# Four buffers for gathered rows instead of two, and all copies of transposed rows on ScalarE, in a fused attention and top-1 expert kernel

## The chip, the cores and the metric

The kernel runs on one core of a Trainium2 chip. A core has five engines that run side by side and wait for each other by semaphores: TensorE (PE, matrix multiplication and transposes; its weight loads are shown apart, as PEld), VectorE (DVE), ScalarE (ACT), GpSimd (POOL) and SyncE (SP, which here only starts transfers). Matrix results arrive in PSUM, which is divided into eight banks; everything else that is computed on lies in SBUF. The metric is the device time of one execution, in microseconds (us).

## The reference

Two blocks are computed one after the other, all in 32-bit floats. First comes linear attention with decay, over 4 batches, 8 heads, 768 positions and heads of 64, in blocks with a running state. Its output, seen as 3072 tokens of 512 numbers, goes through a switch layer: a router picks one of 8 experts for each token, and that expert's two-layer network is applied.

```python
def _moe_ref(x, w_gate, w1, w2):          # x: 3072 x 512, w1: 8 x 512 x 1024, w2: 8 x 1024 x 512
    logits = x @ w_gate
    expert_idx = np.argmax(logits, axis=1)
    probs = softmax(logits)                # written out in the reference
    gate_w = probs[np.arange(N), expert_idx]
    for e in range(E):
        mask = expert_idx == e
        h = np.maximum(x[mask] @ w1[e], 0.0)
        out[mask] = gate_w[mask, None] * (h @ w2[e])
```

## The kernel before

**Attention and routing, 0 to about 140 us.** The positions are taken in six steps of 128, each for two pairs of batches. For each, PE transposes q and k, forms scores, applies them to v and updates the state. The attention output of 128 tokens is copied from PSUM by ACT (xT, line 286), multiplied with a matrix that turns it back and gives the router's logits (lines 319 and 321), copied by ACT again (lg and x, lines 325 and 326) and stored to the DRAM tensor xs. `choose` finds each token's expert. `put` counts with two small matmuls (rank, line 375) the place of each token on its expert's list and writes one entry per token to the DRAM tensor slots, with an indirect transfer from POOL (line 391).

**The expert passes.** The expert part works on lists of tokens in nine passes. Expert 0 is split: pass 0a takes its first 256 tokens, and its turn runs while attention still finishes, and pass 0b takes 136 more. Passes 1 to 7 take one whole expert each, with 424, 408, 408, 384, 368, 368 and 360 tokens. A pass has these steps:

- `fetch` (line 429) gathers the rows of the pass from xs into tiles xg, 128 rows per indirect transfer from POOL (line 437). One tile of xg holds two such blocks of rows, so a pass takes one tile (0a, 0b) or two (1 to 7). The tiles come from a pool with the tag xg.
- `turn` (line 461) transposes the rows on PE: for each of four chunks of 128 features there are one to four transposes into a PSUM bank (tp, line 466; two banks, 0 and 1, in turn), and the bank is then copied to the tile xgT. Copies of chunks 0 and 2 go to DVE (line 453), those of 1 and 3 to ACT (line 451), so chunk 2 waits for the copy of chunk 0, and chunk 3 for that of chunk 1.
- `hidden` (passes 0a and 0b, line 476) or `hidden_fast` (passes 1 to 7, line 552) multiplies with w1. `hidden_fast` uses a Strassen-like scheme of seven products on halves of the operands, in two rounds. It needs sums of halves of w1 (`first_sums`: the tiles s_k, s_q, s_v and one in place of a part of w1t, four POOL operations, lines 513 and 516) and of the tokens (`token_sums`: four DVE operations, lines 506 to 509, named t_sd, xgT, t_x, t_xT). DVE combines the products (lines 489 to 493 and 561), ACT applies the relu (line 563).
- `outputs` (line 611) and, for the first two blocks of 128 tokens of passes 1 to 7, `outputs_fast` (line 580) multiply with w2. The latter needs sums of w2 (`second_sums`: t_q, t_v, t_k, t_m, four POOL operations) and of the hidden values (`pair_sums`: h_qsT, h_qT, h_kT, h_kd, four DVE operations that read SBUF tiles, lines 499 to 502). The second of the seven products of line 580 reads t_k and h_kT.
- `scatter` (line 443) writes the rows to their places in the output, by indirect transfers from POOL.

**What sets the order.** The loop at line 788 works on pass i and prepares the next ones: after `hidden` of a pass come the turn of the next pass, its token sums, the first sums for it, the gathers for the pass after it, the second sums, and then the outputs of the current pass. So the turn of a pass stands between the hidden part and the outputs of the pass before it. Weights of a pass are loaded by SP two passes ahead, when the tiles w1t and w2t come free. The sums of weights share pools with the attention's inputs, three buffers for each of the tags q, k, v, so t_q of a pass takes the buffer that s_q of the pass before held, and can't start before PE is done with that s_q; the same goes for t_v and s_v.

The framework gives out the buffers of a tag in rotation, adds the waits for buffers and data, and reorders instructions within an engine by its own estimate of when they can start, except those that are pinned. Each engine then runs its list in order. With two xg tiles, a gather for the pass after the next waits until the next pass has been turned; on POOL's list everything behind such a gather waits with it.

Of the kernel before, what the change touches and what calls it, by code (L numbers as in the profile page):

```python
# [10 lines left out]
F32 = mybir.dt.float32  # L11
BF16 = mybir.dt.bfloat16
I32 = mybir.dt.int32
# [8 lines left out]
def kernel(  # L22
# [29 lines left out]
    nc = tc.nc  # L52
    B, H, S, D = q.shape
    N, MD = out.shape
    E = moe_w_gate.shape[1]
    F = moe_w1.shape[2]
    P = 128
# [13 lines left out]
    R = N + EARLY + P  # L71
    ENTRY = 4
# [112 lines left out]
    ffn = ctx.enter_context(tc.tile_pool(name="ffn", bufs=2))  # L185
# [3 lines left out]
    def bank(i, shape, name):  # L189
        return ps.tile(shape, F32, tag=f"bank{i}", name=name)  # L190
# [7 lines left out]
    def pin(inst):  # L198
        tc.keep_in_program_order(inst)
# [195 lines left out]
            tc.declare_no_dep(put.ins, group="put", reason="disjoint rows of the lists")  # L395
            tc.add_to_no_dep_group("put", put.ins)

    empty = ffn.tile([P, E * R // P, ENTRY], I32, tag="xg", name="empty", bufs=2)
    nc.gpsimd.memset(empty, 0)
    nc.gpsimd.memset(empty[:, :, 1], N)  # L400

# [18 lines left out]
    def at(m, t):  # L420

        w = m.widths[t]
        return m.ids[:w, t, 0:1], m.ids[:w, t, 1:2], m.list[:w, t, 2:3]
# [5 lines left out]
    def fetch(m, rows=1 + N):  # L429
        m.xg = []  # L430
        for t, w in enumerate(m.widths):
            if t % 2 == 0:
                m.xg.append(ffn.tile([P, 2, MD], F32, tag="xg", name="xg", bufs=2))
            gather(m.xg[-1][:w, t % 2, :], at(m, t)[0], rows)

    def gather(dst, idx, rows):
        nc.gpsimd.indirect_dma_start(  # L437
            out=dst, out_offset=None, in_=xs[:rows, :],
            in_offset=bass.IndirectOffsetOnAxis(ap=idx, axis=0))
# [6 lines left out]
        tc.declare_no_dep(put.ins, group="rows", reason="a token is on one list, once")  # L446
        tc.add_to_no_dep_group("rows", put.ins)

    def evac(i, dst, src):
        if i % 2:  # L450
            nc.scalar.copy(dst, src)
        else:
            nc.vector.tensor_copy(dst, src)

    def relu(i, dst, src):
        if i % 2:
            nc.scalar.activation(dst, src, ACT.Relu)
        else:
            nc.vector.tensor_scalar_max(dst, src, 0.0)  # L459

    def turn(m, pin=lambda inst: inst):
        m.xgT = ffn.tile([P, DC, m.n], F32, tag="xgT", name="xgT", bufs=1)
        for dc in range(DC):
            tp = bank(next(tp_banks), [P, m.n], "tp")
            for t, w in enumerate(m.widths):
                pin(nc.tensor.transpose(tp[:, t * P:t * P + w],  # L466
                                        m.xg[t // 2][:w, t % 2, dc * P:(dc + 1) * P],
                                        ident[:w, :w]))
            evac(dc, m.xgT[:, dc, :], tp)

    def hidden(m, w1t):
        m.hT = ffn.tile([P, FC, m.n], F32, tag="hT", name="hT", bufs=1)
# [215 lines left out]
    def start_early():  # L688

        nc.vector.tensor_scalar(out=skip, in0=had, scalar1=-1.0, scalar2=float(EARLY),  # L690
                                op0=ALU.mult, op1=ALU.add)
        nc.vector.tensor_scalar_max(skip, skip, 0.0)
        base[0] = const.tile([P, E], F32, name="ebase_late")
        nc.vector.tensor_copy(base[0], ebase)
        nc.vector.tensor_add(base[0][:, 0:1], base[0][:, 0:1], skip)
        m = make_pass(0, 0, EARLY, "0a")
        fetch(m, 1 + (NSTEP - 2) * B * C)
        passes.append(m)
# [11 lines left out]
    for i in range(len(order)):  # L710
# [20 lines left out]
        if ahead:  # L731
            for s in range(2):
                score(ahead, s)
        last, cur = cur, ahead
    turn(passes[0], pin)
    give_places(chosen.pop())
    leave(last)
# [47 lines left out]
    for m in passes[1:3]:  # L785
        fetch(m)
    last = len(passes) - 1
    for i, m in enumerate(passes):
        w1t, w2t = weights[max(i - 1, 0)]
        if i < 2:  # L790
            hidden(m, w1t)
        else:
            w1, w2 = w1_next, w2_next
            hidden_fast(m, w1)
        if 0 < i < last:
            turn(passes[i + 1])
            token_sums(passes[i + 1])
            w1_next = first_sums(weights[i][0])
        if 0 < i < last - 1:
            fetch(passes[i + 2])  # L800
        if 0 < i < last:
            w2_next = second_sums(weights[i][1])
        if i == last:

            tc.keep_in_program_order(nc.gpsimd.drain())
        if i < 2:
            outputs(m, w2t)
        else:
            outputs_fast(m, w2t, w2)
        if i == 0:  # L810
            turn(passes[1])
        if 0 < i < last - 1:
            weights.append(load_weights(passes[i + 2].w))
# [3 lines left out]
    with tc.If(most > 0):  # L817
        for i in range(E):
            tiles = nc.values_load(beyond[0:1, i:i + 1], min_val=0, max_val=MORE[i])
            with tc.If(tiles > 0):  # L820
# [4 lines left out]
                with tc.For_i(0, tiles, 1) as r:  # L825
                    m = SimpleNamespace(n=P, widths=[P])
# [36 lines left out]
```

## Time and profile before

| what | value |
|---|---|
| median of three runs | 477.9 us (477.66 to 478.23) |
| the profiled execution's own time | 476.67 us |
| its span, first to last instruction | 474.9 us |
| PE busy | 452.5 us, 95% |
| DVE, ACT, POOL busy | 215.2, 126.6, 247.4 us |
| copies of transposed rows on DVE (line 453) | 18, 9.2 us in all |
| the same on ACT (line 451) | 18, 8.1 us in all |
| gathers (line 437), passes 1 to 7 | 24, 25.8 us busy, 70.1 us idle before them |
| granted TensorE clock, mean | 0.993 |

Times in the text are us from the start of the span of the profiled execution. In a line of the timeline the first number is the start and the second the duration; then come the engine, the line of the kernel, the operation, the tiles written and read, their shapes, and how many instructions of the kind are merged. In square brackets stands how long the engine was idle before it and what ended the idle time. In a list of waits the three numbers are the total in us, how often, and the longest. A turn is named by the pass whose rows it turns: the turns of passes 0a, 0b and 1 to 7 begin on PE at 132.6, 164.6, 173.8, 206.5, 251.2, 294.2, 334.8, 372.7 and 410.5.

### The profile page before, as it was taken

The numbers are of one execution on the slowest core, as the hardware profiler recorded it, in microseconds if no ns is written. First come the engines' busy times: TensorE is split into PE (matmuls) and PEld (weight loads), VectorE is DVE, ScalarE is ACT, GpSimd is POOL, SyncE is SP. The second block draws the span as 40 slices with busy tenths as digits, with TensorE's granted clock in tenths as the row PEclk, the third lists the DMA queues.
The fourth block names the chain that finished last, engine by engine and source line by source line (L and its number), as shares of the span: only waits on it lengthen the run. The fifth ranks groups of instructions, "written<-read, shape, count | busy, mean of one in ns | idle before, by whom it ended". The sixth has DMA issues, their size and how long they took to land.

```text
span 474.9 us, 8613 instructions
## 1 busy us (share of the span) xinstructions
PE 452.5 (95%) x3447; PEld 375.5 (79%) x3447; DVE 215.2 (45%) x495; ACT 126.6 (27%) x323; POOL 247.4 (52%) x190
## 2 busy tenths in 40 slices
PE   5999999999899999999999999999999999999994
PEld 4889898988686475975995799599689689779963
DVE  3753656555433124471245435534623623653421
ACT  3453444544331011220122213112212212211310
POOL 5423535333144749949914970993596398621001
PEclk9999999999899999999999999999999999999998
DMA  9999999998214946441516060542615426001001
GB/s 180 229 268 244 215 241 228 256 303 282 85 54 122 305 153 216 153 181 68 201 48 245 26 222 15 227 141 107 239 41 203 181 78 224 1 20 44 1 17 51
DMA packets 99840, 72.60 MB, mean 153 GB/s; under 512 B 81235, under 2 KB 81239, under 8 KB 99792
## 3 DMA queue, kind: packets, MB, share of 16 engines
q1 hardware_dynamic: 90608, 52.49, 40.1%
q0 software_dynamic: 5008, 13.16, 7.9%
q10 hardware_dynamic: 4176, 6.31, 3.8%
q8 instruction: 29, 0.48, 0.4%
q14 instruction: 19, 0.16, 0.1%
HBM read 58.88 MB, written 13.16 MB: 152 GB/s over the span
## 4 chain that ended last, share of the span: by engine, by line
PE 89%; SPq 3%; DMA 2%; DVE 2%; issue 1%; ACT 1%; POOL 0%; POOLq 0%; ACTq 0%
PE p L552 27%; PE p L580 18%; PE po L611 16%; PE op L277 4%; PE sp L242 4%; PE ph L476 3%; SPq L93 3%; PE tp L466 3%; PE op L265 3%; PE tx L319 2%; PE cp L294 2%; PE tk L207 2%; PE tx L321 2%; PE tq L207 2%; DMA k_in<-in_k_dram 2%
## 5 line engine op out<-in xcount | busy, mean ns | idle before, releaser
L611 PE MATMUL po<-w2t,hT 128*128 128x512 f32 (+5 forms) x224 | 81.0, 596 | 0.0
L437 POOL DMA_INDIRECT xg<-xs,list x24 | 25.8, 1075 | 70.1 <-PE tp L466 64.6
L611 PEld LDWEIGHTS po<-w2t,hT 128*128 128x128 f32 (+5 forms) x224 | 30.5, 162 | 38.2 <-issue 37.9
L563 ACT ACTIVATE hT<-hT 128x408 f32<-128x408 f32 (+4 forms) x56 | 29.5, 527 | 86.7 <-DVE hT L561 86.0
L443 POOL DMA_INDIRECT out_dram<-o,list x24 | 23.8, 990 | 50.9 <-DVE o L617 27.7
L232 POOL TENSOR_TENSOR kd<-k_in,kdec 128x512 f32<-128x512 f32 x20 | 20.7, 1056 | 40.1 <-PE cp L294 22.3
L552 PE MATMUL p<-xgT,w1t 128*128 128x204 f32 (+4 forms) x224 | 41.5, 328 | 0.0
L391 POOL DMA_INDIRECT slots<-entry,slot_i x24 | 23.3, 973 | 31.4 <-DMA w2t<-in_moe_w_dram 12.4
L552 PEld LDWEIGHTS p<-xgT,w1t 128*128 128x128 f32 x224 | 37.6, 190 | 1.2 <-issue 0.9
L248 DVE TENSOR_TENSOR mt<-sp,decay 128x512 f32<-128x512 f32 x48 | 29.8, 682 | 13.8 <-PE sp L242 13.6
L592 DVE SCALAR_TENSOR_TENSOR o<-p,list,o 128x256 f32<-128x256 f32 x28 | 13.5, 484 | 32.9 <-PE p L580 17.0
L277 PE MATMUL op<-mt,v_in 128*64 128x128 f32 x384 | 25.1, 285 | 1.9 <-ACT fence L273 1.9
L580 PE MATMUL p<-w2t,hT 128*128 128x256 f32 x112 | 26.8, 382 | 0.0
L580 PEld LDWEIGHTS p<-w2t,hT 128*128 128x128 f32 x112 | 21.0, 190 | 7.0 <-issue 4.5
L242 PE MATMUL sp<-qT,kT 64*128 64x128 f32 x384 | 25.4, 283 | 0.0
L242 PEld LDWEIGHTS sp<-qT,kT 64*128 64x128 f32 x384 | 23.1, 192 | 1.8 <-issue 1.0
L277 PEld LDWEIGHTS op<-mt,v_in 128*64 128x64 f32 x384 | 22.2, 144 | 2.6 <-ACT fence L273 2.2
L476 PE MATMUL ph<-xgT,w1t 128*128 128x256 f32 (+1 forms) x128 | 22.8, 333 | 0.3 <-DVE hT L459 0.3
L561 DVE TENSOR_TENSOR hT<-p,u_qsT 128x408 f32<-128x408 f32 (+4 forms) x28 | 15.7, 560 | 15.8 <-PE p L552 15.8
L286 ACT COPY xT<-op 128x512 f32<-128x512 f32 x24 | 12.9, 589 | 36.9 <-PE op L265 30.3
L466 PEld LDWEIGHTS tp<-ident,xg 128*128 128x128 f32 (+3 forms) x112 | 13.2, 140 | 10.9 <-issue 3.4
L476 PEld LDWEIGHTS ph<-xgT,w1t 128*128 128x128 f32 x128 | 19.2, 190 | 2.3 <-DVE hT L459 0.7
(163 smaller groups left out, 928.4 us busy)
## 6 DMA issues: line engine op xcount, KB each, us to landing
w1t<-in_moe_w_dram SPq DMA_DIRECT2D x8, 2048.0 KB, 9.0
w2t<-in_moe_w_dram SPq DMA_DIRECT2D x8, 2048.0 KB
v_in<-in_v_dram SPq DMA_DIRECT2D x12, 512.0 KB, 8.0
xs<-x ACTq DMA_DIRECT2D x24, 256.0 KB
q_in<-in_q_dram SPq DMA_DIRECT2D x11, 512.0 KB, 8.3
k_in<-in_k_dram SPq DMA_DIRECT2D x11, 512.0 KB, 9.5
q_in<-in_q_dram SPq DMA_DIRECT2D x2, 256.0 KB
k_in<-in_k_dram SPq DMA_DIRECT2D x2, 256.0 KB
```

What stands on the lines that cost most here:

```text
L242: pin(nc.tensor.matmul(sp[u][:, i, b, :], lhsT=m.kT[s][halves[u], i, b, :], rhs=m.qT[s][halves[u], i, b, :], start=(i == 0 and b == 0), st ...
L248: nc.vector.tensor_mul(mt[:, u], sp[u], decay[:, u, s * HP // 2:(s + 1) * HP // 2].unsqueeze(2).to_broadcast(shp))
L277: pin(nc.tensor.matmul(out_at(m, b, u, hp), lhsT=m.v[:, b, 2 * hp + u, :], rhs=m.mt[hp // 2][:, u, hp % 2, b, :], start=(m.n == 0 and hp = ...
L391: put = nc.gpsimd.indirect_dma_start(out=slots, out_offset=bass.IndirectOffsetOnAxis(ap=slot_i[:, i:i + 1], axis=0), in_=entry[:, n, b, :] ...
L437: nc.gpsimd.indirect_dma_start(out=dst, out_offset=None, in_=xs[:rows, :], in_offset=bass.IndirectOffsetOnAxis(ap=idx, axis=0))
L443: put = nc.gpsimd.indirect_dma_start(out=out, out_offset=bass.IndirectOffsetOnAxis(ap=idx, axis=0), in_=src, in_offset=None, bounds_check= ...
L466: pin(nc.tensor.transpose(tp[:, t * P:t * P + w], m.xg[t // 2][:w, t % 2, dc * P:(dc + 1) * P], ident[:w, :w]))
L476: nc.tensor.matmul(ph, lhsT=w1t[:, dc, fc * P:(fc + 1) * P], rhs=m.xgT[:, dc, :], start=(dc == 0), stop=(dc == DC - 1))
L552: nc.tensor.matmul(p[:, i, :], lhsT=lhs[:, dc, (c + i) * P:(c + i + 1) * P], rhs=rhs[:, dc, :], start=(dc == 0), stop=(dc == DH - 1))
L563: nc.scalar.activation(outs[i][k], outs[i][k], ACT.Relu)
L580: nc.tensor.matmul(p, lhsT=lhs[:, fc, :], rhs=rhs[:, fc, :], start=(fc == 0), stop=(fc == FC // 2 - 1))
L611: nc.tensor.matmul(po[part], lhsT=m.hT[:, fc, t * P:t * P + w], rhs=w2t[:, fc, :], start=(i < k), stop=(i >= FC - k), skip_group_check=True)
```

## The change

The pool tag xg gets four buffers instead of two. The tile `empty`, with which the lists are cleared before they are filled, has the same tag. Apart from that `fetch` stays as it is; since a gather now finds a free tile earlier, the framework places the gathers earlier on POOL's list. On that list the last two of the four gathers of pass 1 now stand before the four weight sums of that pass, and from pass 3 on the gathers of a pass stand directly behind t_m of the sums two passes before it, about a pass earlier than they did. The helper `evac`, which alternated between DVE and ACT, is gone: all four copies of each turn are made by ACT. The order of the other instructions on PE, DVE, ACT and SP stays the same, apart from the transposes of chunks 2 and 3: one transpose of chunk 3 no longer comes before the last one of chunk 2 in some turns.

```diff
-    empty = ffn.tile([P, E * R // P, ENTRY], I32, tag="xg", name="empty", bufs=2)
+    empty = ffn.tile([P, E * R // P, ENTRY], I32, tag="xg", name="empty", bufs=4)
...
             if t % 2 == 0:
-                m.xg.append(ffn.tile([P, 2, MD], F32, tag="xg", name="xg", bufs=2))
+                m.xg.append(ffn.tile([P, 2, MD], F32, tag="xg", name="xg", bufs=4))
             gather(m.xg[-1][:w, t % 2, :], at(m, t)[0], rows)
...
-    def evac(i, dst, src):
-        if i % 2:
-            nc.scalar.copy(dst, src)
-        else:
-            nc.vector.tensor_copy(dst, src)
...
-            evac(dc, m.xgT[:, dc, :], tp)
+
+            nc.scalar.copy(m.xgT[:, dc, :], tp)
```

## The prediction

> **What bounds the kernel now.** I read the page's busy shares and chain first, then the list of waits of TensorE (PE) and GpSimd (POOL), then the timeline around the few places where PE stands still in the expert part (from 132 us on).
>
> ```profile
> PE 452.5 (95%) x3447; PEld 375.5 (79%) x3447; DVE 215.2 (45%) x495; ACT 126.6 (27%) x323; POOL 247.4 (52%) x190
> ...
> PE 89%; SPq 3%; DMA 2%; DVE 2%; issue 1%; ACT 1%; POOL 0%; POOLq 0%; ACTq 0%
> ```
>
> PE is busy 95% of the span and is 89% of the chain that ended last. A change to gathers and copies is worth what PE stops or starts waiting for.
>
> ```profile
> PE tp L466 <- DVE xgT L453: 1.4, 2, 1.1
> PE tp L466 <- DMA xg<-xs,list: 0.9, 1, 0.9
> ...
> POOL xg L437 <- PE tp L466: 64.6, 6, 15.7
> ```
>
> The first two lines are all that the page's waits charge to PE for the work that is changed: 1.4 us for a copy by VectorE (DVE), 0.9 us for gathered rows. The third is large, but it is POOL that waits: gathers wait for a turn to free their buffer. Off the chain that costs nothing by itself; it does decide what POOL runs beside the turn.
>
> The one late gather is that of the last 168 rows of pass 1:
>
> ```profile
> 170.44 0.99 POOL L437 DMA_INDIRECT xg<-xs,list  x1 [0.30 <-PE ph L476]
> ...
> 173.79 0.49 PE L466 MATMUL tp<-ident,xg 128*128 128x128 f32 x3
> 175.18 0.91 PE L466 MATMUL tp<-ident,xg 40*128 40x40 f32 x5 [0.89 <-DMA xg<-xs,list]
> ```
>
> The turn of pass 7 is the other place. No gather stands before it on POOL, so the weight sums t_v, t_k, t_m run during the turn; before it, the turn of pass 6 has gathers there instead:
>
> ```profile
> 409.53 2.36 POOL L516 TENSOR_TENSOR t_v<-w2t 128x1024 f32<-128x1024 f32 x1 [2.63 <-PE p L552]
> 410.53 0.79 PE L466 MATMUL tp<-ident,xg 128*128 128x128 f32 x6
> 410.61 1.83 DVE L499 TENSOR_TENSOR h_qsT<-hT 128x512 f32<-128x512 f32 x1 [0.58 <-ACT hT L563]
> 411.84 2.81 POOL L516 TENSOR_TENSOR t_k<-w2t,t_q 128x1024 f32<-128x1024 f32 x1
> 412.81 0.52 DVE L453 COPY xgT<-tp 128x360 f32<-128x360 f32 x1
> 413.38 0.73 PE L466 MATMUL tp<-ident,xg 128*128 128x128 f32 x5 [1.09 <-DVE xgT L453]
> 414.73 2.51 POOL L516 TENSOR_TENSOR t_m<-w2t,t_k 128x1024 f32<-128x1024 f32 x1
> 414.96 2.83 DVE L500 TENSOR_TENSOR h_qT<-hT 128x512 f32<-128x512 f32 x1
> 418.16 0.68 DVE L501 TENSOR_TENSOR h_kT<-h_qT,hT 128x512 f32<-128x512 f32 x1
> 419.97 1.89 PE L580 MATMUL p<-w2t,hT 128*128 128x256 f32 x8
> ```
> ```profile
> 372.68 0.80 PE L466 MATMUL tp<-ident,xg 128*128 128x128 f32 x6
> 372.75 0.69 DVE L499 TENSOR_TENSOR h_qsT<-hT 128x512 f32<-128x512 f32 x1 [0.57 <-ACT hT L563]
> 380.99 1.89 PE L580 MATMUL p<-w2t,hT 128*128 128x256 f32 x8
> ```
>
> The reader is to see two things. DVE operations that read two SBUF tiles take 1.83 and 2.83 us beside POOL's sums against 0.69 without, and each ends soon after a POOL operation ends: they take turns. And PE paid for it only through the copy xgT that stood behind h_qsT on DVE: from first transpose to L580, 9.44 us (410.53 to 419.97) against 8.31 us (372.68 to 380.99).
>
> **The change, part by part.** The sum is made against the profiled execution (476.67 us, a span of 474.9 and 1.8 around it), and then carried to the median of 477.9, which lies 1.2 us higher.
>
> *Buffers, gathers earlier.* Two more tiles of 4 KB a partition. The number of gathers, sums and scatters is the same, and so is SP's order. On POOL the last two gathers of pass 1 move from behind its four weight sums to before them; those of pass 2 come between and behind the scatters of 0a; from pass 3 on, the gathers of a pass stand about one pass earlier. (1) The stall of pass 1 goes. From 173.79 to the 30 L611 matmuls at 178.25 is 4.46 us; the same stretch of pass 2's turn is 3.42 (206.46 to 209.88): −1.04 us, between −0.9 (the wait alone) and −1.1. What is moved past: two gathers at 0.99 + 0.94 + 0.6 of gaps put s_k at 158.0 or, if they take transfer time from w1t, about 1 us later. The sums of pass 1 then end at about 169 instead of 167.7, and PE first uses s_q at 187.8: hidden by 18 us. For all later passes the gathers were hidden already (pass 7's are issued by 379.5, used at 410.5): 0.
>
> *What POOL does instead of waiting.* With no gather in the way, t_q starts as soon as PE is done with the s_q whose buffer it takes, as at 404.55 in pass 7's stretch, and t_v when PE is done with s_v, 1.0 us before the turn (409.53 to 410.53). So t_v, t_k, t_m fall on the turns of passes 2 to 6 too, five collisions that are new. (2) Their cost on PE: the copies, through which the turn of pass 7 paid, leave DVE. Next in line is h_kT, wanted by the second L580 group. In the turn of pass 7 it ended at 418.84, 8.3 us after the first transpose; about 0.4 us of that is a copy (417.72) that leaves, so 7.9. PE wants it 12 transposes, 16 L611 and 8 L580 matmuls after the first transpose, 8.31 + 1.73 = 10.0 us less a stall of 0.15 below: 9.9. Slack 2.0 us at the turns of 5, 6 and 7, more where 32 L611 matmuls follow. I take 0. Bounds: 0 and 1.13 each as once measured, 5.65 in all.
>
> The same pair of engines is a subject of the Trainium skill, "SBUF — State Buffer", section "SBUF: two separate sides": VectorE operations with two SBUF inputs and GpSimd share a port pair as an exclusive lock, and the loser waits the whole instruction. The rows agree as far as they go. Read as a rule against the change, five turns with three waits of at most 2.36 us each would hold DVE back by an estimated 35 us at most, and with all of it on PE the sum would be +33; by the rows, PE stands for none of it while h_kT has slack, and the sum is −2.0.
>
> *All 36 copies by ScalarE (ACT).* DVE loses 18 copies (9.2 us busy), ACT gains 18 (its 18 are 8.1 us). ACT is 27% busy, but its queue is in order. (3) Turn of pass 7: its wait for DVE goes. ACT can take the first copy at about 411.1 and the second at 411.56, done 412.02, when PE ends its two L611: −1.13 (9.44 to 8.31); bounds −0.6, if part of it returns behind ACT's relu, and −1.13. (4) In turns 4 to 6 the second six transposes take 0.80 us against 0.65 for the first, for a bank that DVE frees late (374.34); ACT frees both by about 374.0 while PE is in L611 till 374.18. 0.15 each in four turns with pass 7's, and about 0.1 in those of passes 2 and 3: up to −0.8, I take −0.65; the bounds are 0 and −0.9.
>
> What ACT makes late: the first turns, where it is not free.
>
> ```profile
> 132.62 1.07 ACT L286 COPY xT<-op 128x512 f32<-128x512 f32 x2 [2.45 <-PE op L265]
> 133.58 0.39 ACT L451 COPY xgT<-tp 128x256 f32<-128x256 f32 x1
> ```
>
> (5) Turn of 0a: DVE copied the first block at 133.02, and PE went on at 133.50. Now that copy stands behind two xT copies, 133.58 to 133.97, and PE goes on at about 134.02: +0.52. Queued behind PE's wait are the rank matmuls and the sixteen L319/L321 that feed the router, so the whole stretch to the end shifts; the later waits there (0.4 at 138.74, 0.3 at 145.57) hang on the same chain and absorb nothing. Bounds 0.3 and 0.8. (6) Turn of 0b: ACT is in an L615 of 0.69 us till 165.47, so the first copy starts at 165.38 instead of 165.05 on DVE: +0.30; bounds 0.1 and 0.5. Later turns find ACT idle. Behind each turn's copies on ACT stands one relu (L563) and then L615 of a tile 5 us or more away.
>
> One rule speaks against this part: the Trainium skill, "TensorEngine Tiling (Array Packing)", section "PSUM Bottleneck", advises to use both ScalarE and VectorE to empty PSUM. It has no figure; if each of nine turns lost what (5) loses, the sum would have +4.7 in place of +0.82. The rows show ACT idle for 0.7 us or more before its copies in the later turns, so only two turns pay.
>
> Sum: −1.04 − 1.13 − 0.65 + 0.52 + 0.30 + 0 = −2.0 us. 474.7 for the profiled kind of execution, 475.9 beside the median. With the bounds of (1) and (3) to (6): −0.9 − 0.6 + 0 + 1.3 = −0.2, and −1.1 − 1.13 − 0.9 + 0.4 = −2.7: 475.2 to 477.7.
>
> **The rivals.** *The port collisions reach PE (slower).* Place: L580 of passes 1 to 5, the second group, which needs h_kT. If each of the five new collisions costs what the one in the trace did, 5 × 1.13 = 5.65 with (1), (5) and (6) is +5.4: 483.3; if only the turns of 5 and 6 pay, with their short outputs, 2 × 1.13 and (1), (5), (6) give +2.0: 479.9. For it: 2.83 us for h_qT. Against: the path through DVE's copies is gone. It decides from where h_kT ends more than 9.9 us after the first transpose; t_q may come 2.6 us late (it ended 406.9, t_v started 409.53) before anything shifts, and 2.0 more before PE waits. w2t, landing like w1t in 7.6 to 13.5 us from an issue at 391.63, would be there at 405.1 at worst.
>
> *Gains and losses cancel (no change).* Gathers were hidden but for one, and ACT's queue gives that one back: −1.04 + 0.82 with (3) and (4) lost to the relu that stands between ACT's copies and waits for DVE's last hT (412.89 in pass 7's turn): 477.7. Against: only the third and fourth copies are behind that relu, and PE's next need of their banks is a pass away.
>
> *ACT becomes the bound in the early turns (slower by little).* If the router's chain at 132 to 139 loses 2 us instead of 0.52, with (3) and (4) also halved: −1.04 − 0.9 + 2.3 = +0.4, up to 479. Against: ACT had idle gaps of 0.66, 0.23 and 0.40 us there.
>
> **How the numbers follow.** A difference of 0.2% (0.95 us) is about what a measurement of this kernel can tell from none. Forecast 0.66; cancelling 0.13; collisions 0.16; early turns 0.05. Predicted 475.9, its own range 475.2 to 477.7. Faster 0.67 (nearly all of the forecast, a little of the cancelling case), same 0.12, slower 0.21. The range goes to 474.9 below and to 479.5 above, which leaves out about 0.07 below and the dear half of the collisions above.
>
> **What the profile after would show.** (1) No PE wait on gathered rows; pass 1's turn to L611 in 3.4 us. (2) h_qsT, t_sd and h_qT between 1 and 3 us in six turns, with no PE wait in L580. (3), (4) no PE wait at L466 of the late turns; the stretch of pass 7 about 8.2 us. (5), (6) new PE waits on ACT at 134 and 165.7 of about 0.8 and 0.3 us. POOL no longer waits 64.6 us in gathers; it waits for PE's L552 before t_q and t_v. Wrong would be: waits of L580 on DVE's h_kT, or a longer router stretch.

## The result, and the profile after

| what | before | after |
|---|---|---|
| median, first measurement (22 runs each, in turn on one chip) | 478.36 us | 477.15 us |
| ratio after to before, 95% interval | | 0.9973 (0.9960 to 0.9986) |
| second measurement | 478.97 us | 477.17 us, 0.9945 (0.9925 to 0.9964) |
| third, on another chip than the second | 473.73 us | 470.66 us, 0.9956 (0.9925 to 0.9987) |
| the profiled execution's own time, its span | 476.67, 474.9 us | 476.91, 475.1 us |
| TensorE (PE), VectorE (DVE), ScalarE (ACT), GpSimd (POOL) busy | 452.5, 215.2, 126.6, 247.4 us | 451.0, 238.2, 133.1, 251.0 us |

The change makes the kernel faster, by 1.2 us in the first measurement and by 1.8 and 3.1 us in the two later ones. The profiled execution of after shows nothing of that in its span. Its attention part, which the change does not touch, was 1.39 us later: the turn of 0a begins at 133.95 instead of 132.56. From the turn of 0a to the last group of matmuls after takes 332.43 us and before 333.80, 1.37 less. So all comparisons of traces below go by stretches within the expert part, and all verdicts on times by the ratios with their intervals. A ratio is the one on record for its measurement; it is not the quotient of the two medians beside it, from which it differs by up to 0.3%. Of before there is one trace. In the two later executions of after the stretch from the turn of 0a to the last group takes 332.55 and 331.49 us, 1.25 and 2.31 less than in that trace.

The lines of line 449 and later have moved up by 5: L611 is now L606, L580 is L575, L466 is L460, L552 is L547, L516 is L511, L499 to L502 are L494 to L497, L506 to L509 are L501 to L504, L617 is L612, and the copies of transposed rows are all in L464. Of the page of after, the busy times and the chain that ended last:

```profile
PE 451.0 (95%) x3447; PEld 374.6 (79%) x3447; DVE 238.2 (50%) x477; ACT 133.1 (28%) x341; POOL 251.0 (53%) x190
...
PE 89%; DMA 3%; SPq 3%; ACT 1%; issue 1%; another core or an unknown queue 0%; DVE 0%; POOLq 0%; POOL 0%; ACTq 0%
```

DVE has 18 copies less and yet 23.0 us more busy time. That is the first sign of the collisions with POOL, and PE does not show them. The list of waits of after, with PE's waits in the expert part and one of POOL (total, how often, longest):

```profile
PE rank L375 <- DVE sm L357: 1.2, 1, 1.2
PE tp L460 <- ACT xgT L464: 1.1, 2, 0.8
...
POOL t_q L511 <- PE p L547: 39.9, 5, 9.0
```

PE no longer waits for gathered rows, nor for DVE's copies in late turns. It waits for ACT in the turns of 0a and 0b, and 1.2 us for the router, which is new. POOL now stands before the sums of w2, not before gathers: its gathers have 6.6 us of idle time before them, where it was 70.1. The timeline at the turn of pass 7:

```profile
410.85 2.36 POOL L511 TENSOR_TENSOR t_v<-w2t 128x1024 f32<-128x1024 f32 x1 [2.63 <-PE p L547]
411.85 0.79 PE L460 MATMUL tp<-ident,xg 128*128 128x128 f32 x6
411.93 1.83 DVE L494 TENSOR_TENSOR h_qsT<-hT 128x512 f32<-128x512 f32 x1 [0.58 <-ACT hT L558]
412.36 0.82 ACT L464 COPY xgT<-tp 128x360 f32<-128x360 f32 x2 [0.47 <-PE tp L460]
413.34 0.79 PE L460 MATMUL tp<-ident,xg 128*128 128x128 f32 x6
416.29 2.83 DVE L495 TENSOR_TENSOR h_qT<-hT 128x512 f32<-128x512 f32 x1
419.16 0.69 DVE L496 TENSOR_TENSOR h_kT<-h_qT,hT 128x512 f32<-128x512 f32 x1
419.98 1.89 PE L575 MATMUL p<-w2t,hT 128*128 128x256 f32 x8
421.71 1.89 PE L575 MATMUL p<-t_k,h_kT 128*128 128x256 f32 x8
```

The collision is still there (1.83 and 2.83 us), but the second six transposes start without a wait, because ACT copies beside it. From the first transpose to L575 it is 8.13 us (411.85 to 419.98) instead of 9.44. h_kT ends at 419.85, 1.86 us before the group that reads it.

Two tables hold nearly all that follows. The first is of the late part: from the 30 matmuls of L606 in the turn of pass 1 to the start of the last group of L575 (L611 and L580 in the old numbering), as the timelines of the profiled executions have it. The executions named a second or third time are those of the experiments below.

| version | late part, us |
|---|---|
| before | 288.11 |
| after, three executions | 286.34, 286.34, 286.34 |
| ACT copies, two buffers (two executions) | 286.34, 286.34 |
| the four other versions below with ACT's copies from pass 1 on and the sums of w2 as in before or after | 286.34 to 286.35 |
| four buffers alone | 292.52 |
| t_m computed twice | 291.54 |
| three buffers | 311.06 |

The second is of the early part: the stretch from the first transpose of 0a to the first L606, and that from the first transpose of pass 1 to the 30 L606.

| version | copies in 0a and 0b | 0a, us | turn of pass 1, us |
|---|---|---|---|
| before | DVE and ACT | 18.29 | 4.46 |
| after, three executions | ACT | 19.37, 19.36, 18.43 | 3.49, 3.62, 3.48 |
| ACT copies, two buffers (two executions) | ACT | 19.31, 20.53 | 3.49, 3.49 |
| three buffers | ACT | 18.23 | 3.49 |
| four buffers alone | DVE and ACT | 17.67 | 4.56 |
| four buffers, 0a and 0b copied by both | DVE and ACT | 18.29 | 4.61 |
| own buffer for 0b (two executions) | DVE and ACT | 18.38, 21.18 | 3.49, 3.49 |
| two buffers, 0a and 0b copied by both | DVE and ACT | 20.25 | 3.49 |
| relu swapped | ACT | 18.38 | 4.72 |
| t_m computed twice | ACT | 19.36 | 3.64 |

The late part is the same to 0.01 us from execution to execution, and the early part is not. What the change is worth with certainty lies in the late part, 288.11 - 286.34 = 1.77 us.

### The profile page after: what moved, and what is told of

Read it like the earlier page. It is cut to its first block, busy times and chain, and to the rows that moved or that the text cites. A ratio compares the mean times of both kernels' runs of the same rounds, so it can differ in the third digit from the quotient of the medians.

```text
span 475.1 us, 8604 instructions
## 1 busy us (share of the span) xinstructions
PE 451.0 (95%) x3447; PEld 374.6 (79%) x3447; DVE 238.2 (50%) x477; ACT 133.1 (28%) x341; POOL 251.0 (53%) x190
## 4 chain that ended last, share of the span: by engine, by line
PE 89%; DMA 3%; SPq 3%; ACT 1%; issue 1%; another core or an unknown queue 0%; DVE 0%; POOLq 0%; POOL 0%; ACTq 0%
PE p L547 27%; PE p L575 18%; PE po L606 17%; PE ph L471 5%; PE sp L242 4%; PE op L277 4%; DMA k_in<-in_k_dram 3%; SPq L93 3%; PE tp L460 3%; PE op L265 3%; PE tx L319 2%; PE tk L207 2%; PE tx L321 2%; PE cp L294 2%; PE tq L207 2%
## 5 line engine op out<-in xcount | busy, mean ns | idle before, releaser
L606 PE MATMUL po<-w2t,hT 128*128 128x512 f32 (+5 forms) x224 | 81.0, 596 | 0.0
L606 PEld LDWEIGHTS po<-w2t,hT 128*128 128x128 f32 (+5 forms) x224 | 30.5, 162 | 38.2 <-issue 37.7
L547 PE MATMUL p<-xgT,w1t 128*128 128x204 f32 (+4 forms) x224 | 41.5, 328 | 0.0
L547 PEld LDWEIGHTS p<-xgT,w1t 128*128 128x128 f32 x224 | 37.6, 190 | 1.2 <-issue 0.9
L511 POOL TENSOR_TENSOR t_q<-w2t 128x1024 f32<-128x1024 f32 x7 | 16.5, 2357 | 39.9 <-PE p L547 39.9
L575 PE MATMUL p<-w2t,hT 128*128 128x256 f32 x112 | 26.8, 382 | 0.0
L575 PEld LDWEIGHTS p<-w2t,hT 128*128 128x128 f32 x112 | 21.0, 190 | 7.0 <-issue 4.5
L277 PE MATMUL op<-mt,v_in 128*64 128x128 f32 x384 | 23.8, 274 | 2.6 <-ACT fence L273 2.5
L511 POOL TENSOR_TENSOR t_v<-w2t 128x1024 f32<-128x1024 f32 x7 | 16.5, 2361 | 16.0 <-PE p L547 16.0
L277 PEld LDWEIGHTS op<-mt,v_in 128*64 128x64 f32 x384 | 20.8, 137 | 3.6 <-ACT fence L273 3.1
```

Source lines behind the costliest of these rows:

```text
L277: pin(nc.tensor.matmul(out_at(m, b, u, hp), lhsT=m.v[:, b, 2 * hp + u, :], rhs=m.mt[hp // 2][:, u, hp % 2, b, :], start=(m.n == 0 and hp = ...
L511: return nc.gpsimd.tensor_tensor(out=o, in0=x, in1=y, op=ALU.subtract)
L547: nc.tensor.matmul(p[:, i, :], lhsT=lhs[:, dc, (c + i) * P:(c + i + 1) * P], rhs=rhs[:, dc, :], start=(dc == 0), stop=(dc == DH - 1))
L575: nc.tensor.matmul(p, lhsT=lhs[:, fc, :], rhs=rhs[:, fc, :], start=(fc == 0), stop=(fc == FC // 2 - 1))
L606: nc.tensor.matmul(po[part], lhsT=m.hT[:, fc, t * P:t * P + w], rhs=w2t[:, fc, :], start=(i < k), stop=(i >= FC - k), skip_group_check=True)
```

## The experiments

The theory was the prediction's: of the two parts of the change, ACT's copies take PE off a path that POOL's sums block, the earlier gathers are worth one late transfer, and the collisions that they bring stay hidden behind the slack of h_kT. The rivals were that the collisions reach PE, and that the buffers do no harm by themselves.

### Four buffers alone

```diff
-    empty = ffn.tile([P, E * R // P, ENTRY], I32, tag="xg", name="empty", bufs=2)
+    empty = ffn.tile([P, E * R // P, ENTRY], I32, tag="xg", name="empty", bufs=4)
...
-                m.xg.append(ffn.tile([P, 2, MD], F32, tag="xg", name="xg", bufs=2))
+                m.xg.append(ffn.tile([P, 2, MD], F32, tag="xg", name="xg", bufs=4))
```

> Four buffers, but the copies of transposed rows still alternate between DVE and ACT. My theory: the weight sums of POOL now fall on the turns of passes 2 to 7, and each turn pays what the turn of pass 7 paid before, 1.13 us by way of the copy that stands behind h_qsT on DVE; the late gather of pass 1 (1.04 us) goes: 5 x 1.13 - 1.04 = +4.6 us against before, a ratio near 1.010. Rival: earlier gathers do no harm and bring their 1.04 us: ratio 0.998.

Measured: 482.25 us beside 477.42, a ratio of 1.013 (1.0098 to 1.0162). The profiled execution took 481.17 us. Its late part is 4.41 us longer than before's, in the turns of passes 2 to 6 by 0.53, 0.55, 1.07, 1.12 and 1.14. The list of PE's waits, and the timeline at the turn of pass 6, which had no such wait before:

```profile
PE tp L466 <- DVE xgT L453: 6.0, 8, 1.1
```
```profile
376.07 1.83 DVE L499 TENSOR_TENSOR h_qsT<-hT 128x512 f32<-128x512 f32 x1 [0.58 <-ACT hT L563]
377.31 2.81 POOL L516 TENSOR_TENSOR t_k<-w2t,t_q 128x1024 f32<-128x1024 f32 x1
378.28 0.52 DVE L453 COPY xgT<-tp 128x368 f32<-128x368 f32 x1
378.86 0.75 PE L466 MATMUL tp<-ident,xg 128*128 128x128 f32 x5 [1.09 <-DVE xgT L453]
```

This is the wait of pass 7, now in the turn of pass 6. Each turn from 4 on pays what the trace of before showed for one, and those of 2 and 3 pay half. So far the theory holds; that the buffers are harmless alone is refuted. Its other half did not come: PE reaches the turn of pass 1 at 173.74, as early as before, and no longer waits for rows, but the turn takes 4.56 us instead of 4.46. Another wait has taken the place of that for rows:

```profile
176.98 1.39 PE L466 MATMUL tp<-ident,xg 128*128 128x128 f32 x8 [0.86 <-DVE xgT L453]
```

DVE's and ACT's first copies stand here behind relus of 0b that start at 176.04 and 176.14, of which more below. Three of the six runs took 483 to 485.8 us, more than the trace explains; why is open.

### ACT's copies alone

```diff
-    empty = ffn.tile([P, E * R // P, ENTRY], I32, tag="xg", name="empty", bufs=4)
+    empty = ffn.tile([P, E * R // P, ENTRY], I32, tag="xg", name="empty", bufs=2)
...
-                m.xg.append(ffn.tile([P, 2, MD], F32, tag="xg", name="xg", bufs=4))
+                m.xg.append(ffn.tile([P, 2, MD], F32, tag="xg", name="xg", bufs=2))
```

This is the changed kernel with two buffers, so the old helper is gone and all copies are ACT's.

> Two buffers, all copies on ACT. My theory: the turn of pass 7 gains 1.3 us, those of 4 to 6 0.15 each, the turns of 0a and 0b lose 0.52 and 0.30, and the stretch of 0a to its first L606 loses 0.56 more, as in the changed kernel; the gather of pass 1 stays late: -1.3 - 0.45 + 0.82 + 0.56 = -0.4 us against before, ratio 0.999. Rival for the 0.56 us: it does not hang on the copies (but on the buffers, or on chance), then -0.9 us, ratio 0.998, and no longer stretch of 0a than 18.8 us from its first transpose to its first L606.

> Two buffers, all copies on ACT, once more, beside the changed kernel on one chip. If the two more buffers bring nothing as soon as ACT makes the copies, both have the same time within 0.1%, 1.4 us less than before (ratio 0.997); if the buffers are worth their 1.0 us, this one is 0.2% slower than the changed kernel.

Measured: 475.19 us beside 477.42, 0.9966 (0.9952 to 0.998), and beside the third measurement of the changed kernel 471.79 beside 473.73, 0.996 (0.9933 to 0.9987), where the changed kernel had 470.66. The worth of the buffers, 1.0 us, was expected to be missing, and nothing is. The timeline of the first of these executions at the turn of pass 1:

```profile
171.82 0.94 POOL L437 DMA_INDIRECT xg<-xs,list  x1 [0.30 <-issue]
175.75 1.33 PE L460 MATMUL tp<-ident,xg 128*128 128x128 f32 x8
177.01 1.12 PE L606 MATMUL po<-w2t,hT 128*128 128x512 f32 x2
```

The last gather is issued 0.1 us later than before (171.73), but PE comes to the turn at 175.75 and not at 173.79, and no longer waits for the rows. In before PE stood until 175.18 for them. Of the 1.96 us 0.65 are from the attention part and 1.31 from the stretches of 0a and 0b, which ACT's copies lengthen; these alone are more than the 0.89 us that PE waited. So the late gather and the losses of ACT in the early turns were not two terms to add: they run side by side, and PE pays the longer. Once ACT makes the copies of 0a and 0b too, the two more buffers bring nothing that can be measured.

### Three buffers

```diff
-    empty = ffn.tile([P, E * R // P, ENTRY], I32, tag="xg", name="empty", bufs=4)
+    empty = ffn.tile([P, E * R // P, ENTRY], I32, tag="xg", name="empty", bufs=3)
...
-                m.xg.append(ffn.tile([P, 2, MD], F32, tag="xg", name="xg", bufs=4))
+                m.xg.append(ffn.tile([P, 2, MD], F32, tag="xg", name="xg", bufs=3))
```

> Three buffers instead of four, all copies on ACT. My theory: the only gather that ever was late is that of the last rows of pass 1; a third buffer is enough for it, and whatever else POOL does stays off PE's path: the changed kernel's time, 1.3 us less than before, ratio 0.997. Rival: gathers now stand between t_k and t_m and hold back t_m, or a gather is late again: up to 1 us slower than the changed kernel, ratio 0.999.

Measured: 498.27 us beside 477.42, 1.0465 (1.0434 to 1.0497). Both expectations are wrong by more than 20 us. What PE waits for in the late part, and the timeline at the turn of pass 5:

```profile
PE p L575 <- DVE o L612: 15.1, 4, 4.0
```
```profile
347.03 0.97 POOL L437 DMA_INDIRECT xg<-xs,list  x1 [17.11 <-PE tp L460]
347.72 7.66 DVE L502 TENSOR_TENSOR xgT<-xgT 128x368 f32<-128x368 f32 x1
348.00 2.37 POOL L511 TENSOR_TENSOR t_q<-w2t 128x1024 f32<-128x1024 f32 x1
350.31 2.37 POOL L511 TENSOR_TENSOR t_v<-w2t 128x1024 f32<-128x1024 f32 x1
352.62 2.36 POOL L511 TENSOR_TENSOR t_k<-w2t,t_q 128x1024 f32<-128x1024 f32 x1
359.55 0.74 DVE L612 TENSOR_SCALAR o<-po,list 128x512 f32<-128x512 f32 x1
360.35 3.78 PE L575 MATMUL p<-t_v,h_qsT 128*128 128x256 f32 x8 [4.01 <-DVE o L612]
```

A gather that finds no free tile stands before t_q and waits for the turn, 17.1 us; then t_q, t_v and t_k come in one row behind it, and one DVE operation of some 0.55 us lasts 7.66. h_kT was done before that row began. What came late is the copy o of the third tile (L612) behind it on DVE: it frees the PSUM bank that the third group of L575 writes. (Where the pass has four tiles, at the turns of 3 and 4, it is the second group that waits for L612.) PE waits 4.01 us here, and it then runs slower: the granted clock is 0.50 from 358.85 to 365.67, and the third group takes 3.78 us, where it is 1.89 in after. The turns of 3 to 6 pay 5.5 to 6.9 us each, 24.7 in all. Of these 15.1 are PE's waits, and 9.7 are longer busy time of PE, which is at half its clock for 20.5 us of them. So the rival "the collisions reach PE" is real; what decides is where on POOL's list the gathers stand, and the bank behind L612, not h_kT, is what breaks.

### One more POOL operation beside the turns

```diff
-        return right_sums(b, t1, t2, t3, t4, pool_sub_last)
+        r = right_sums(b, t1, t2, t3, t4, pool_sub_last); pool_sub_last(t4, b[1][0], t2); return r
```

> The changed kernel with t_m computed twice, one more POOL operation of 2.36 us that reads SBUF beside the turns. DVE's operations behind h_qsT come up to 2.4 us later. By the prediction's slack (h_kT is next, 1.9 us before PE needs it) PE waits 0.5 us in the turns of 5, 6 and 7: +1.5 us against the changed kernel. What the run with three buffers suggests: next is not h_kT but the copy o of the third tile (L612), which frees the bank that the third group of L575 needs; it ends 0.98 us before that in the turn of 6: waits of 1.4 us there and in 5 and 7, up to 0.3 in 3 and 4: +4.2 to +5 us. If DVE gets its turn between any two POOL operations: no change.

Measured: 481.61 us beside 478.97, 1.006 (1.0032 to 1.0088), 4.4 us above the changed kernel's 477.17 on the same chip. The late part grows by 5.20 us. The timeline at the turn of pass 6:

```profile
381.48 5.28 POOL L511 TENSOR_TENSOR t_m<-w2t,t_k 128x1024 f32<-128x1024 f32 x2
384.59 2.73 DVE L496 TENSOR_TENSOR h_kT<-h_qT,hT 128x512 f32<-128x512 f32 x1
387.46 1.97 PE L575 MATMUL p<-t_k,h_kT 128*128 128x256 f32 x8
389.20 0.74 DVE L612 TENSOR_SCALAR o<-po,list 112x512 f32<-112x512 f32 x1
389.99 1.99 PE L575 MATMUL p<-t_v,h_qsT 128*128 128x256 f32 x8 [0.56 <-DVE o L612]
```

h_kT ends at 387.32 and its group starts at 387.46, 2.03 us after the first and not 1.73, so its slack is used up, as the prediction counted it, and costs 0.30 us. PE then waits 0.56 us for the bank freed by L612. From the first group of L575 (385.43) to the third it is 4.56 us instead of 3.46. The turns of 5, 6 and 7 pay 1.14, 1.21 and 1.18. Of the three expectations that of the bank comes nearest: its place is right, and its size there, 1.4 us, a little high. It missed the turn of 4, which pays 1.47 where at most 0.3 was expected: the pass there has four tiles, and the bank is wanted one group earlier. h_kT alone would give 1.5 us in all, and a fair change of turns between the two engines nothing.

### Both engines in the turns of 0a and 0b

The changed kernel, with this at the copies:

```diff
-            nc.scalar.copy(m.xgT[:, dc, :], tp)
+            copy = nc.vector.tensor_copy if P < m.n <= 2 * P and dc % 2 == 0 else nc.scalar.copy
+            copy(m.xgT[:, dc, :], tp)
```

> The changed kernel, but in the turns of 0a and 0b chunks 0 and 2 are copied by DVE again. My theory: the waits of PE for ACT at those turns (0.52 and 0.30) go, and with them the later relu of the first hidden block that stood between key and pick on DVE (0.56): 1.4 us less than the changed kernel, 2.7 less than before, ratio to before 0.9945. Rival: the 0.56 us have another cause, or the router's chain waits for something else next: 0.8 us less than the changed kernel, ratio to before 0.9955. If ACT was no bound there at all: the ratio of the changed kernel, 0.997.

Measured: 476.29 us beside 477.42, 0.9979 (0.9962 to 0.9995), no better than the changed kernel in its first measurement (0.9973). The first half of the theory holds: the stretch of 0a is 18.29 us, to the hundredth that of before, and the one from the turn of 0b to that of pass 1 is 9.21 (before 9.21, after 9.50). But the turn of pass 1 takes 4.61 us instead of 3.49. Its timeline:

```profile
174.25 0.97 POOL L437 DMA_INDIRECT xg<-xs,list  x1 [0.30 <-issue]
175.05 1.34 PE L460 MATMUL tp<-ident,xg 128*128 128x128 f32 x8
175.52 0.90 POOL L437 DMA_INDIRECT xg<-xs,list  x1 [0.30 <-issue]
177.60 0.28 ACT L451 ACTIVATE hT<-ph 128x136 f32<-128x136 f32 x1 [2.65 <-PE tp L460]
177.78 0.93 ACT L464 COPY xgT<-tp 128x424 f32<-128x424 f32 x2
178.34 1.39 PE L460 MATMUL tp<-ident,xg 128*128 128x128 f32 x8 [0.90 <-ACT xgT L464]
179.66 8.11 PE L606 MATMUL po<-w2t,hT 128*128 128x512 f32 x30
```

ACT's copies stand behind the last relu of 0b (L451), and that relu starts at 177.60, although PE's last matmul for it starts at 174.9. By the profile it is a signal of PE that the relu waits for, and it comes late, in a stretch in which POOL issues the gathers of pass 2 one behind the other. What the copies of 0a and 0b gave back was lost again here, to a wait that only an early PE meets.

### A buffer of its own for 0b

```diff
-                m.xg.append(ffn.tile([P, 2, MD], F32, tag="xg", name="xg", bufs=4))
+                own = P < m.n < EARLY; m.xg.append(ffn.tile([P, 2, MD], F32, tag="xg0b" if own else "xg", name="xg", bufs=1 if own else 2))
```

Together with the edit of the copies of the experiment before, and `empty` with two buffers. The gathers of pass 1 are early, as in the changed kernel, and those of pass 2 and later wait for the turn, as in before.

> Two shared buffers again, and one of its own for the rows of pass 0b; in the turns of 0a and 0b chunks 0 and 2 are copied by DVE, everywhere else all four by ACT. So the gathers of pass 1 come before its weight sums, those of pass 2 and later stay behind the turn, and POOL's sums of w2 do not meet a turn before that of pass 7. My theory: the stretches of 0a and 0b are as before, the turn of pass 1 loses its wait for rows (1.04 us) and nothing takes its place, since the gathers of pass 2 no longer run beside the hidden part of 0b; turns 4 to 7 keep their gain (1.3 + 0.45 us): 2.8 us less than before, 1.4 less than the changed kernel, ratio to before 0.994. Rival: the relu that held up ACT's copies in the turn of pass 1 is late for another reason than the gathers beside it, and 0.9 us stay lost there: ratio 0.996.

> The version with two shared buffers and one of its own for 0b, once more: 2.6 us less than before by its first trace, ratio 0.9945, and 0.25% less than the changed kernel. Rival: what it gains behind 0a is lost in the spread of the attention part, and it can't be told from the changed kernel.

Measured: 476.52 us beside 478.97, 0.9945 (0.9923 to 0.9966), and beside the third measurement 471.7 beside 473.73, 0.9947 (0.9919 to 0.9976). The same turn, at nearly the same time as in the version before:

```profile
174.99 1.34 PE L460 MATMUL tp<-ident,xg 128*128 128x128 f32 x8
175.19 0.28 ACT L451 ACTIVATE hT<-ph 128x136 f32<-128x136 f32 x1 [1.57 <-PE ph L471]
175.75 1.13 ACT L464 COPY xgT<-tp 128x424 f32<-128x424 f32 x2 [0.27 <-PE tp L460]
177.22 1.33 PE L460 MATMUL tp<-ident,xg 128*128 128x128 f32 x8
178.48 8.11 PE L606 MATMUL po<-w2t,hT 128*128 128x512 f32 x30
178.53 0.98 POOL L437 DMA_INDIRECT xg<-xs,list  x1 [7.16 <-PE tp L460]
```

Between the two versions only POOL's gathers and the sums behind them have moved, and the relu starts at 175.19 and not at 177.60. The two ran on different chips, but each chip has the contrast by itself: beside the four gathers of pass 2 the last relu is late there in all five executions, with none or two of them it is in time in all three. So on these chips the gathers, or the transfers that they start, go with the late relu, as the theory has it. It is no rule: in the third execution of the changed kernel, on yet another chip, the relu was in time beside the same gathers. There the last of them ended 0.75 us before the end of PE's last matmul for the relu; in the six late executions it ended from 0.30 us before that to 1.2 us after it. Whether that is the reason was not tried. From the turn of 0a to the last group this execution takes 331.16 us, 2.64 less than before and 1.27 less than after. As a time that is not to be seen: 476.52 beside the changed kernel's 477.17, and 471.7 beside 470.66. In the second execution the 0a stretch is 21.18 us: PE came to it early, stood 2.2 and 1.1 us for its rows, and was then granted half its clock (0.50 from 127.8 to 134.6 us). The second rival, that it can't be told from the changed kernel, holds.

### The relu of 0a swapped between DVE and ACT

```diff
-            relu(fc, m.hT[:, fc, :], ph)
+            relu(fc + (m.n == EARLY), m.hT[:, fc, :], ph)
```

> The changed kernel, but in pass 0a the relu of hidden blocks 0, 2, 4, 6 is done by ACT and that of 1, 3, 5, 7 by DVE, so that no relu stands between key and pick on DVE. My theory: the extra loss in the stretch of 0a comes from that relu, for which the signal of PE came 1.2 us late; PE's wait of 1.2 us for the router goes, and the stretch from the first transpose to the first L606 falls from 19.37 to about 18.3 us: 0.5 to 1.1 us less than the changed kernel, ratio to before 0.995 to 0.996. Rival: the router itself is late behind ACT's copies; the stretch stays at 19.3 us and the time is that of the changed kernel, ratio 0.997.

In the timeline of after the extra loss behind 0a looks like this:

```profile
139.62 0.18 DVE L344 SCALAR_TENSOR_TENSOR key<-sh,rev 128x16 f32<-128x16 f32 x1
141.00 0.42 DVE L453 TENSOR_SCALAR hT<-ph 128x256 f32<-128x256 f32 x1 [1.20 <-PE ph L471]
141.34 0.16 DVE L348 TENSOR_REDUCE pick<-key 128x2 f32<-128x16 f32 x1
141.85 0.17 PE L375 MATMUL rank<-oh,before 128*128 128x16 bf16 x1 [1.20 <-DVE sm L357]
```

And with the relu moved out of DVE's way:

```profile
135.66 0.44 PE L460 MATMUL tp<-ident,xg 128*128 128x128 f32 x2 [0.82 <-ACT xgT L464]
139.87 0.18 DVE L344 SCALAR_TENSOR_TENSOR key<-sh,rev 128x16 f32<-128x16 f32 x1
140.09 0.17 DVE L348 TENSOR_REDUCE pick<-key 128x2 f32<-128x16 f32 x1
140.74 0.17 PE L375 MATMUL rank<-oh,before 128*128 128x16 bf16 x1
```

The stretch falls to 18.38 us, 0.99 less than after, though PE still waits 0.82 us for ACT's first copies. So the late relu between key and pick costs the 1.2 us wait, as the theory has it. The time is 477.8 us beside 478.97, 0.9982 (0.996 to 1.0005): no gain, because the turn of pass 1 is 4.72 us again, with a wait of 1.01 us for ACT.

### Two buffers, both engines in 0a and 0b

The version with the own buffer, without it: the edit of the copies, and two buffers.

> Two buffers, DVE and ACT in turn for the copies of 0a and 0b as before the change, all copies on ACT from pass 1 on. It is the version with a buffer of its own for 0b, without that buffer. My theory: TensorE reaches the turn of pass 1 as early as before the change, so the late gather is back: the stretch from the first transpose of that turn to the 30 L606 is 4.4 us instead of 3.5; the turns of 4 to 7 keep their 1.7 us: from the first transpose of 0a to the end 1.8 us less than before, ratio 0.996, and 0.9 us more than the version with the own buffer. Rival: the buffer is worth nothing here either; no PE wait for rows and the time of that version.

Measured: 472.44 us beside 473.73, 0.9961 (0.9929 to 0.9992). The time is as expected, but the reason can't be read: on this chip PE waited 1.9 us for the rows of 0a, ran at a granted clock of 0.50 for a while after that, and came so late to pass 1 that its turn has no wait (3.49 us). Whether the own buffer is worth 1 us when PE is early is not settled by this. The first execution with that buffer speaks for it: PE came to pass 1 41.33 us after the start of the turn of 0a, in before 41.23, and had no wait for rows.

The changed kernel itself was measured twice more, beside the versions with the swapped relu and the second sum, and beside the one with two buffers and both engines:

> The changed kernel itself, on the chip on which the others of this call run, to compare them with. If my account of its parts holds it is 1.4 us faster than before, as its first measurement: ratio 0.997.

> The changed kernel, third measurement, as the measure for the other three of this call: ratio 0.997 to before.

Both are in the first table, at 0.9945 and 0.9956, below 0.997. The second interval (0.9925 to 0.9987) holds 0.997 and the first (0.9925 to 0.9964) just does not. The late part is again 286.34 us; the second trace is 1.25 us shorter than that of before from 0a on, and the third 2.31. There is no trace of before on those chips, so what the rest is stays open.

## Why the prediction was right

The forecast was 475.9 us, 2.0 less than the 477.9 then known, a ratio of 0.9958, and its range was 474.9 to 479.5. The first measurement gives 477.15 and 0.9973, the later two 0.9945 and 0.9956. Sign and size are right, the size in part by luck, as (1), (2) and (5) show. By its steps:

- **(3) and (4), the late turns.** Predicted -1.13 and -0.65, together -1.78. Measured -1.77. The turn of pass 7 gave 1.30, the turns of 4 to 6 gave 0.15 to 0.17 each, and those of 2 and 3 nothing where 0.1 each was allowed. It is the whole certain gain of the change, and two buffers have it too.
- **(2), the collisions.** Right that they come in all turns from pass 2 on and that PE pays nothing: h_qsT takes 1.73 to 1.83 us, h_qT 2.83, and the late part is that of two buffers to the hundredth. One more than the five came, in the turn of pass 1, where t_sd takes 4.79 us; it costs PE nothing either. h_kT had 1.9 us of slack; 2.0 was predicted. Wrong was "Next in line is h_kT". Nearest is the copy o of the third tile, which frees a PSUM bank; in the turn of pass 6 it ended at 384.79, and the third group of L575 started at 385.77, a slack of 0.98 us. One more POOL operation went through it, and three buffers far more. The forecast stood on half the margin that it counted, and that this was enough was luck.
- **(1), the late gather.** The wait is gone and the stretch is 0.97 us shorter, predicted 1.04. But it is not the buffers' doing alone. They do take the wait for rows away, as four buffers alone show, but that stretch is still 4.56 us, by the wait for late relus; and with two buffers and ACT's copies it is 3.49 us as well. The step took PE's arrival at the turn as fixed. Relative to 0a PE came 1.3 us later there, by (5) and (6), and that alone covers the wait of 0.9.
- **(5), the turn of 0a.** PE's wait for ACT is 0.82 us instead of 0.30, +0.52 as predicted. The term is wrong all the same: the stretch became 1.08 us longer. Its words "the later waits there hang on the same chain and absorb nothing" failed both ways. Where the relu on DVE came in time (three buffers) or stood elsewhere (the swapped relu) the stretch is 18.23 and 18.38 us beside 18.29, so the 0.52 were absorbed. Where it came late between key and pick, PE waited 1.2 us more. And the 0.4 us at 138.74 is idle time of the weight loads; PE's own row has no wait there.
- **(6), the turn of 0b.** Predicted +0.30, measured +0.29.
- **The sum.** +1.08 + 0.29 - 0.97 - 1.77 = -1.37 us between the two traces from 0a on, beside -2.0. The difference is (5) almost alone. By the third execution of after, in which the relu of 0a was in time, it is -2.31.

The rival that ends slower, collisions that reach PE, did not come, but it was near: four buffers alone cost 4.41 us in the late part and three with ACT's copies 24.7. "Gains and losses cancel" describes the early part: its losses (1.37 us) and the gather saved (0.97) nearly do. The rule that VectorE and ScalarE should both empty PSUM (the Trainium skill, "TensorEngine Tiling (Array Packing)", section "PSUM Bottleneck"), which the page gives for matmuls sped up by tiling the array, is not borne out here: in the late turns ScalarE alone is faster by 1.77 us, because VectorE is the engine that is held up.

## What to carry to other kernels

A buffer moves more than its own transfer: list what stands behind the transfer on its queue, and see beside which work that now falls. The same two tiles were worth +4.4 us, nothing, or, as one tile instead of two, +24.7, by where POOL's sums came to lie. When an engine is to be held up within its slack, follow all that stands on its list to the next reader, the release of PSUM banks included, and take the smallest margin. Waits that lie on two chains which meet again are not added: the later one counts, and shortening the other only uncovers it.

## What the runs showed of the hardware

- **DVE can wait for a whole row of POOL operations.** The Trainium skill, "SBUF — State Buffer", section "SBUF: two separate sides", says that the port pair shared by VectorE and GpSimd is held for the whole instruction by whoever starts first. The runs agree that one waits for the other and show more: beside three POOL sums in a row (348.00 to 354.98) one DVE operation with two SBUF inputs stayed 7.66 us, over all three. By the profile it had started 0.28 us before the first of them, so by its records it is not the one that started first that went first. At other places DVE came in after one of them (1.83 and 2.83 us) or after two (4.79 us for t_sd in the turn of pass 1 of after). What decides is open.
- **PE's signals can come 1.2 to 2.4 us late,** as far as the profile tells, which models the ends of matmuls. In 0b the last relu starts 7.49 us after the start of PE's row of 62 matmuls in before, with three buffers, and in all versions with two shared buffers. It starts 8.7 to 9.9 us after it in six of the seven executions with four buffers, and there 1.2 to 1.5 us after the end of POOL's last gather; in the seventh it was in time. In 0a the same order of instructions had the first relu in time in three executions and about 1.2 us late in four. So the order of instructions alone does not decide it. Whether the exact times of the gathers do, and by what path a gather would delay a semaphore, is open.
- **PE's granted clock can fall to one half after a stand of 2 to 4 us.** Where PE stood for 0a's rows (0.7 to 2.2 us before the first transpose and 1.0 to 1.1 before the second block, in three executions on one chip) the granted clock was 0.50 for 3.4 to 6.8 us after it. With waits of 1.2 and 0.57 it stayed at 1.00. Together with the second wait it made the 0a stretch up to 2.8 us longer (18.38 and 21.18 us with the own buffer). With three buffers it was 0.50 for 3.4 or 6.8 us about each of the four waits of 3.5 to 4.0 us. But in the attention part it was 0.50 for 3.4 us at a stand of 1.93 us in before (120.61), and stayed at 1.00 at one of 2.54 us in after (122.69). So the length of a stand does not decide it; what does is open.
- **The late part is repeatable to 0.01 us** over ten executions of six versions, while the part from the turn of 0a to it differed by 2.8 us between two executions of one version (44.82 and 47.62). A change of 0.3% is better read from such a stretch than from the span.
